# mLSTM cell and leaky-ReLU feed-forward: chunk 1 scales q on GpSimd and turns it on TensorE, k takes the gate in place of v, and chunk 0 is gated out of PSUM

## The chip, the core and the metric

One core of one Trainium2 chip runs the kernel. The metric is the device time of a run in microseconds, lower is better; the median of three runs of the kernel before is 541.46 us (541.23 to 542.38). A core has five engines that run their own instruction streams in order: TensorE (PE, with its weight loads shown apart as PEld), VectorE (DVE), ScalarE (ACT), GpSimd (POOL) and SyncE (SP), which here issues nearly all transfers. They wait for each other by semaphores. On-chip data lie in SBUF, and TensorE's results in PSUM.

## The reference

Two blocks, one after the other. The first is an mLSTM cell, batch 4, 8 heads, 768 time steps, head size 40, in f32:

```python
m_new = max(f[t] + m, i[t])                       # running maximum, per batch and head
C = exp(f[t] + m - m_new) * C + exp(i[t] - m_new) * outer(v[t], k[t])
n = exp(f[t] + m - m_new) * n + exp(i[t] - m_new) * k[t]
y[t] = sigmoid(o[t]) * (C @ q[t]) / max(|n . q[t]|, 1)
```

The second takes y as 3072 tokens of 320: `h = x @ w_in` (320 x 2048), `g = max(0.01 * h, h)`, `out = g @ w_out` (2048 x 320). The two weights come in as 64-bit floats and are turned into 32-bit ones on the chip.

## The kernel before, in words

**Chunks and steps.** The 768 time steps are cut into 6 chunks c of 128 tokens. A step s = 4 c + b is chunk c of batch b, all 8 heads; so steps 0 to 3 are chunk 0, and 4 to 7 are chunk 1. From chunk 1 on, a step's 128 tokens are two halves u of 64. A step's work on TensorE has two parts. `u_parts` makes the scores k^T q of each half (L576) and the half's contribution to the state, k^T (v times a gate) (L581); VectorE multiplies the scores by the decay matrix w (L586) and adds the contribution to the state (`state_add`, L560). Then `u_plain` (chunk 1) or `u_mix` (chunks 2 to 5) multiplies queries and weighted scores with state and values (hN, L629, or pT, L659), divides by the normaliser (L595 to L597) and applies the output gate (L640, L645). The tile `mixed(s)` holds, for each half, the weighted scores in 64 partitions and the scaled, turned q in 40 of the others, so that one matmul multiplies both with `S_v`, which holds v of the half and the state in the same way, 21 values per row of 32.

**q and k in chunk 1.** `u_split` turns k and q on TensorE by 32 small matmuls with the identity (L498), and ScalarE copies them out of PSUM (L504, four copies) to `kqT`. `prep_kq` (L484, VectorE, two instructions) multiplies the turned q by `ea`, the exponential gate per token, which must lie along the free axis in all partitions: it is written to DRAM by L298 and read back broadcast, two transfers of 128 KB a step (`spread_q`, L403). In later chunks `prep_kq` also turns k and q by VectorE transposes (L478).

**The gate of the state.** `prep_vu` (L458, GpSimd, two instructions of 64 x 336) multiplies v by exp(...) per token; the gate comes from `gT`, where `gates_T` has the gates turned to one column per batch and head (L310). GpSimd also scales the old state (`state_next`, L556) and adds the mask to w (`prep_mask`, L429).

**Chunk 0.** `u_values` multiplies values by weights into PSUM (pa, L604), VectorE copies this to `hn` (L605) and takes the denominators; `gate` (L614) reads `hn`.

**Weights.** `load_weights(n)` loads n = 0 to 3 (quarters of w_in) and n = 4 to 11 (eighths of w_out, 640 KB each), `narrow_weights` turns each to f32 by one ScalarE instruction (L231) and six on VectorE (L233, L237, L241, L243, L245, L247). They are issued in slices between the other work of chunk 0 and chunk 1, two to four per unit.

**The order.** On the four compute engines the program's order is the order written out by hand. While the feed-forward of chunk c - 1 runs as `ff_units` (for chunk 1's loop: 14 halves of L723, then 16 parts of four L758, i = 0 to 29), the cell work of chunk c is put between its units: in the loop of c = 1, `place` puts u_parts of steps 4, 5, 6, 7 behind units 2, 7, 12, 18, u_plain behind 5, 10, 15, 21, the gates of chunk 2 (`u_gates`, tg) behind 16, and the four `u_x` (which turn the result to be the next input, xt) behind 22 to 28. Narrowing comes before a unit, `ahead(s + 1)` after a step's u_plain: u_split, the exponentials of w (`prep_exp`, L437, three before each unit and the rest at u_parts), prep_kq, the loads of step s + 3, state_next, prep_vu, and the mask of the next step. L731 is the leaky ReLU on ScalarE; it frees the two PSUM banks of a unit. SP's queue is ordered by the scheduler, and at most eight transfers are under way: each waits for the one eight before it.

**PSUM.** The pool `psc` (tag c) has four banks for all cell work; a new tile takes the bank that was given up first, and TensorE waits for its last reader.

Of the kernel before, what the change touches and what calls it, by code (L numbers as in the profile page):

```python
# [18 lines left out]
def kernel(  # L19
# [26 lines left out]
    nc = tc.nc  # L46
# [239 lines left out]
    def gates_exp(c):  # L286
        bu, a, na = bus[c]
        if c == 0:
            nc.scalar.activation(bu[:, 1, :], bu[:, 0, :], AF.Exp, bias=a[:BH, P - 1 :], scale=1.0)
            return  # L290
        for u in range(2):
            at = ts(u, SL)
            last = SL * (u + 1) - 1
            nc.scalar.activation(bu[:, 2, at], a[:, at], AF.Exp, bias=na[:] if u else 0.0, scale=1.0)
            nc.scalar.activation(bu[:, 1, at], bu[:, 0, at], AF.Exp, bias=a[:, last : last + 1], scale=1.0)
        if c > 0:
            nc.sync.dma_start(a_dr[c, 0].rearrange("u n t -> n u t"), a[:].rearrange("n (u t) -> n u t", u=2))
# [9 lines left out]
    def gates_T(c, bu):  # L307
        tg = psc.tile([P, 4, BH], F32, name="tg", tag="c")
        for n in range(2):
            nc.tensor.transpose(tg[:, n, :], bu[:, n, :], ident[:BH, :BH])  # L310
        gT[c] = wk.tile([P, 2, BH], F32, name="gT")
        if c > 0:
            for u in range(2):
                last = SL * (u + 1) - 1
                nc.tensor.matmul(
                    tg[:, 2 + u, :], lhsT=bu[:, 2, last : last + 1].to_broadcast([BH, P]), rhs=ident[:BH, :BH],
                    start=True, stop=True,
                )
            gL[c] = f0[:, ts(c % 2, 2 * BH)].rearrange("p (u n) -> p u n", u=2)
        nc.vector.tensor_copy(gT[c][:], tg[:, :2, :])  # L320
        if c > 0:
            nc.vector.tensor_copy(gL[c], tg[:, 2:, :])
# [116 lines left out]
    def prep_vu(s):  # L439
# [3 lines left out]
        if s < NS:  # L443
# [11 lines left out]
            else:  # L455
                for u in range(2 if c + 1 < NB else 1):
                    rows = ts(u, SL)
                    nc.gpsimd.tensor_tensor(  # L458
                        d["vu"][rows], S_v[s % NL][rows, u, :, :, :V1], g[rows].to_broadcast([SL, H, 2, V1]), op=ALU.mult,
                    )  # L460
# [10 lines left out]
    def prep_kq(s):  # L471

        d = st[s]
        n_r = D if s < 2 * B else SL
        if s >= 2 * B:
            d["kqT"] = wk.tile([P, 2, PR * P], F32, name="kqT")
        for i in range(2 if s >= 2 * B else 0):
# [4 lines left out]
        for r in range(2):  # L482
            rows = slice(SL * r, SL * r + n_r)
            nc.vector.tensor_tensor(  # L484
                mixed(s)[rows, 1 - r], d["kqT"][rows, 1].rearrange("p (h t) -> p h t", t=SL), d["ea"][rows], op=ALU.mult,
            )

# [74 lines left out]
    def u_parts(s):  # L562
        c, b = divmod(s, B)
        d = st[s]
        kqT, w = d["kqT"], d["w"]
        run(lazy.pop(s))
# [7 lines left out]
        for h in range(H):  # L574
# [24 lines left out]
    def u_values(s):  # L599
        d = st[s]  # L600
        hn = d["hn"] = wk.tile([P, H, D1], F32, name="hn")
        pa = psc.tile([P, H, D1], F32, name="pa", tag="c")
        for h in range(H):
            nc.tensor.matmul(pa[:, h, :], lhsT=d["w"][:, h, :], rhs=d["va"][:, h, :D1], start=True, stop=True)  # L604
        nc.vector.tensor_copy(hn[:], pa[:])  # L605
        d["den"] = wk.tile([P, H], F32, name="den")
        denominators(d["den"][:], hn[:, :, D])

    def gate(s):
# [5 lines left out]
            x3, in0=d["o"].rearrange("p (h d) -> p h d", d=D), scalar=1.0, in1=d["hn"][:, :, :D],  # L615
# [181 lines left out]
    def ahead(s):  # L797

        if s < NS:
# [188 lines left out]
```

## Time and profile before

| what | value |
|---|---|
| median of three runs | 541.46 us (541.23 to 542.38) |
| profiled execution | 542.91 us, of which the span of the page is 541.1 us |
| chunk 0 on TensorE (first matmul to the start of unit 0) | 1.5 to 52.8 us |
| loop of chunk 1 | 52.8 to 149.0 us |
| loops of chunks 2 to 5 and the last feed-forward | 149.0 to 541.1 us |
| mean granted TensorE clock | 0.962 |

The profile is of one execution. The page gives busy time per engine, and the span in 40 equal slices (13.5 us each) with the busy share in tenths, TensorE's granted clock and the share of the transfer engines. Views of the trace add the instructions in order of time, busy time by stretches, the waits and who ended them, and the chain of work that ended last. L numbers are lines of the kernel before; a shape 128x320 is partitions by elements. Each f32 matmul instruction stands as two records. A busy engine need not be the bound, and an idle one matters only if the end waits for it.

### The profile page before, as it was taken

Reading aid. Unit: us, or ns where it says so; the run is one execution under the profiler, and the core shown is the slowest. Engines: PE = TensorE matmul, PEld = TensorE weight load, DVE = VectorE, ACT = ScalarE, POOL = GpSimd, SP = SyncE. Lnnn points to the kernel's source line nnn. Section 1 sums busy time; section 2 is a strip of 40 time slices with the busy share of each in tenths; the row PEclk is TensorE's granted clock in tenths of the full one; section 3 lists DMA queues with packets and bytes.
Section 4 is the critical chain, followed back from the end, with each engine's and each line's share of the span. In section 5 each row is a group of like instructions: output and inputs, shape, how many; then the busy total and the mean of one; then the engine's idle time right before and its main releaser. Section 6 shows DMA issues by size and latency. Waiting matters only on the chain.

```text
span 541.1 us, 11162 instructions
## 1 busy us (share of the span) xinstructions
PE 523.1 (97%) x4372; PEld 339.3 (63%) x4372; DVE 249.8 (46%) x443; ACT 163.3 (30%) x450; POOL 120.4 (22%) x157
## 2 busy tenths in 40 slices
PE   7989969979999999999999999999999999999997
PEld 7877858756745477645577645567654577644675
DVE  4688896999635536135527135625034532000000
ACT  4566653533433320034220043310043400022100
POOL 4134352252303332103333003423002100000000
PEclk9658988979999999999999999999999999999999
DMA  9976687977525555564655554556531121100000
GB/s 116 165 202 150 158 202 196 185 169 145 129 68 105 124 139 128 135 130 92 128 144 129 143 121 98 129 142 141 123 100 51 50 84 34 42 1 0 13 12 24
DMA packets 166003, 60.18 MB, mean 111 GB/s; under 512 B 129024, under 2 KB 156224, under 8 KB 165952
## 3 DMA queue, kind: packets, MB, share of 16 engines
q1 hardware_dynamic: 165568, 59.35, 49.6%
q8 instruction: 34, 0.56, 0.4%
q10 hardware_dynamic: 384, 0.13, 0.1%
q14 instruction: 17, 0.14, 0.1%
HBM read 52.72 MB, written 6.72 MB: 110 GB/s over the span
## 4 chain that ended last, share of the span: by engine, by line
PE 86%; DVE 6%; DMA 3%; SPq 2%; ACT 1%; issue 1%; POOL 1%; DVEq 0%; POOLq 0%; ACTq 0%
PE ph L723 37%; PE po L758 36%; PE pT L659 3%; PE sd L576 3%; DMA S<-in_v_dram 1%; PE warm L305 1%; PE sd L581 1%; PE pa L604 1%; DMA raw<-in_moe_w_out_dram 1%; PE sc L524 1%; ACT w L437 1%; PE ab L416 1%; POOL vu L458 1%; PE tkq L512 1%; DVE qn L586 1%
## 5 line engine op out<-in xcount | busy, mean ns | idle before, releaser
L723 PE MATMUL ph<-xT,w_in 64*128 64x512 f32 (+1 forms) x1120 | 218.9, 542 | 0.1
L758 PE MATMUL po<-w_out,acts 128*128 128x320 f32 x768 | 216.2, 440 | 0.0
L758 PEld LDWEIGHTS po<-w_out,acts 128*128 128x128 f32 x768 | 145.8, 193 | 60.7 <-issue 4.0
L723 PEld LDWEIGHTS ph<-xT,w_in 64*128 64x128 f32 x1120 | 108.4, 191 | 91.0 <-issue 84.2
L731 ACT ACTIVATE acts<-ph 128x512 f32<-128x512 f32 (+1 forms) x112 | 54.0, 534 | 153.6 <-PE ph L723 153.5
L586 DVE TENSOR_TENSOR qn<-w,sd 64x512 f32<-64x512 f32 x40 | 27.4, 685 | 122.7 <-PE sd L581 87.8
L556 POOL TENSOR_TENSOR S<-S,f 40x336 f32<-40x336 f32 x36 | 28.8, 800 | 181.3 <-PE pT L659 135.9
L437 ACT ACTIVATE w<-w,gT 128x64 f32<-128x64 f32 (+1 forms) x192 | 52.4, 350 | 1.0 <-DVE w L423 1.0
L484 DVE TENSOR_TENSOR qn<-kqT,ea 64x512 f32<-64x512 f32 (+1 forms) x40 | 30.2, 755 | 4.7 <-ACT kqT L504 3.4
L458 POOL TENSOR_TENSOR vu<-S,gT 64x336 f32<-64x336 f32 x36 | 31.4, 871 | 2.7
L673 POOL TENSOR_TENSOR xb<-xb,den 128x320 f32<-128x320 f32 x16 | 11.6, 727 | 88.5 <-DVE xb L670 88.5
L766 ACT COPY y<-po 128x320 f32<-128x320 f32 x12 | 5.1, 425 | 86.7 <-PE po L758 86.7
L766 ACT COPY hn<-po 128x320 f32<-128x320 f32 x12 | 5.1, 425 | 86.3 <-PE po L758 86.3
L576 PEld LDWEIGHTS sd<-kqT 40*64 40x64 f32 x640 | 21.1, 138 | 12.8 <-issue 10.5
L666 DVE STREAM_TRANSPOSE hb<-pT 128x512 f32<-128x512 f32 x16 | 11.5, 717 | 38.1 <-PE pT L659 38.1
L429 POOL TENSOR_TENSOR w<-w,i 128x512 f32<-128x512 f32 x20 | 27.3, 1365 | 7.9 <-ACT acts L731 6.5
L581 PE MATMUL sd<-vu,kn 64*40 64x42 f32 x576 | 21.2, 218 | 4.0 <-POOL vu L458 4.0
L576 PE MATMUL sd<-kqT 40*64 40x64 f32 x640 | 24.2, 225 | 0.4 <-DVE S L560 0.2
L659 PEld LDWEIGHTS pT<-qn,S 128*64 128x64 f32 x512 | 16.2, 138 | 10.5 <-issue 6.9
L581 PEld LDWEIGHTS sd<-vu,kn 64*40 64x40 f32 x576 | 18.6, 114 | 4.2 <-POOL vu L458 4.2
L677 DVE STREAM_TRANSPOSE x<-xb 128x512 f32<-128x512 f32 x16 | 17.7, 1104 | 7.8 <-POOL xb L673 7.8
L478 DVE STREAM_TRANSPOSE kqT<-rb 128x512 f32<-128x512 f32 x32 | 20.6, 680 | 0.0
(123 smaller groups left out, 362.4 us busy)
## 6 DMA issues: line engine op xcount, KB each, us to landing
w<-a_dr SPq DMA_DIRECT2D x40, 128.0 KB
ea<-a_dr SPq DMA_DIRECT2D x40, 128.0 KB
rb<-in_k_dram SPq DMA_DIRECT2D x64, 80.0 KB
rb<-in_q_dram SPq DMA_DIRECT2D x64, 80.0 KB
rb<-in_o_gate_dram SPq DMA_DIRECT2D x64, 80.0 KB
kn<-in_k_dram SPq DMA_DIRECT2D x24, 160.0 KB
raw<-in_moe_w_out_dram SPq DMA_DIRECT2D x6, 640.0 KB
S<-in_v_dram SPq DMA_DIRECT2D x80, 40.0 KB
```

Source lines behind the costliest of these rows:

```text
L429: nc.gpsimd.tensor_tensor(w, w, cm2.unsqueeze(1).to_broadcast([P, H, SL]), op=ALU.add)
L437: yield nc.scalar.activation(w[:, h, :], w[:, h, :], AF.Exp, bias=gT[c][:, 0, bh : bh + 1], scale=1.0)
L458: nc.gpsimd.tensor_tensor(d["vu"][rows], S_v[s % NL][rows, u, :, :, :V1], g[rows].to_broadcast([SL, H, 2, V1]), op=ALU.mult,)
L484: nc.vector.tensor_tensor(mixed(s)[rows, 1 - r], d["kqT"][rows, 1].rearrange("p (h t) -> p h t", t=SL), d["ea"][rows], op=ALU.mult,)
L556: nc.gpsimd.tensor_tensor(new, old, g, op=ALU.mult)
L576: nc.tensor.matmul(bank[1 - u][toks, h, :], lhsT=kqT[rows, 0, ts(h, SL)], rhs=kqT[rows, 1, ts(h, SL)], start=True, stop=True,)
L581: nc.tensor.matmul(dC[u][:, h].rearrange("p k d -> p (k d)"), lhsT=d["k"][toks, h, :D], rhs=d["vu"][toks, h].rearrange("p k d -> p (k d)") ...
L586: nc.vector.tensor_tensor(mixed(s)[toks, u], w[toks], bank[1 - u][toks], op=ALU.mult)
L659: nc.tensor.matmul(pT[DP * r : DP * (r + 1), j * P + u * SL : j * P + (u + 1) * SL], lhsT=S[:, u, h, :], rhs=m[:, u, h, :], start=True, st ...
L723: nc.tensor.matmul(ph[r][:, cols], lhsT=w_row(r, slot, j), rhs=xT[DP * r : DP * (r + 1), slot, cols], start=(slot == 0), stop=(slot == KC ...
L731: nc.scalar.activation(acts[:, f, cols], ph[r][:, cols], AF.Prelu, alpha=0.01)
L758: nc.tensor.matmul(po[n][:], lhsT=acts[:, f, ts(n, P)], rhs=w_out[:, f, :], start=(f == 0), stop=(f == NF - 1),)
```

## The change

- In chunk 1 the gate that was `ea` is turned by `gates_T` as a third kind into `gT`. `prep_qs` (GpSimd) multiplies the rows of q, as loaded, by it, into a tile of the ring `y`; `split_qs` (TensorE, 16 matmuls with the identity, into two more tiles of the pool) turns them at the start of u_parts, and ScalarE copies both halves into `mixed(s)`. VectorE's product, the transfers of `ea` for steps 4 to 7 and the write of that gate to DRAM go.
- From chunk 1 on, k and not v takes the gate of the state: one GpSimd product 128 x 320 in place of two of 64 x 336; the matmul takes v in place from `S_v`.
- In chunk 0, denominators and gate read pa in PSUM; the copy to `hn` goes.

```diff
@@ gates_exp
-            nc.sync.dma_start(a_dr[c, 1].rearrange("u n t -> n u t"), bu[:, 2, :].rearrange("n (u t) -> n u t", u=2))
+            if c > 1:
+                nc.sync.dma_start(a_dr[c, 1].rearrange("u n t -> n u t"), bu[:, 2, :].rearrange("n (u t) -> n u t", u=2))
@@ gates_T
-        tg = psc.tile([P, 4, BH], F32, name="tg", tag="c")
-        for n in range(2):
+        tg = psc.tile([P, 5, BH], F32, name="tg", tag="c")
+        kinds = 3 if c == 1 else 2
+        for n in range(kinds):
             nc.tensor.transpose(tg[:, n, :], bu[:, n, :], ident[:BH, :BH])
...
-        nc.vector.tensor_copy(gT[c][:], tg[:, :2, :])
+        nc.vector.tensor_copy(gT[c][:, :kinds], tg[:, :kinds, :])
@@ prep_vu
-                for u in range(2 if c + 1 < NB else 1):
-                    rows = ts(u, SL)
-                    nc.gpsimd.tensor_tensor(
-                        d["vu"][rows], S_v[s % NL][rows, u, :, :, :V1], g[rows].to_broadcast([SL, H, 2, V1]), op=ALU.mult,
-                    )
+                d["ku"] = d["vu"][:].rearrange("p h k d -> p (h k d)")[:, : H * D].rearrange("p (h d) -> p h d", d=D)
+                nc.gpsimd.tensor_tensor(
+                    d["ku"], d["k"][:, :, :D], gT[c][:, 1, ts(b, H)].unsqueeze(2).to_broadcast([P, H, D]), op=ALU.mult,
+                )
+
+    def prep_qs(s):
+        c, b = divmod(s, B)
+        d = st[s]
+        d["qs"] = wk.tile([P, Dm], F32, name="y")[:].rearrange("p (h d) -> p h d", d=D)
+        nc.gpsimd.tensor_tensor(
+            d["qs"], natural(s, 1), gT[c][:, 2, ts(b, H)].unsqueeze(2).to_broadcast([P, H, D]), op=ALU.mult,
+        )
@@ after prep_kq (which now serves chunks 2 to 5 alone)
+    def split_qs(s):
+        tq = [psc.tile([P, H, SL], F32, name=f"tq{u}", tag="c") for u in range(2)]
+        for h in range(H):
+            for u, toks, rows in subs(s):
+                nc.tensor.matmul(tq[u][rows, h, :], lhsT=st[s]["qs"][toks, h], rhs=ident[toks, toks], start=True, stop=True)
+        for u, toks, rows in subs(s):
+            nc.scalar.copy(mixed(s)[rows, u], tq[u][rows])
@@ u_parts
+        if c == 1:
+            split_qs(s)
         run(lazy.pop(s))
...
-                        dC[u][:, h].rearrange("p k d -> p (k d)"), lhsT=d["k"][toks, h, :D],
-                        rhs=d["vu"][toks, h].rearrange("p k d -> p (k d)"), start=True, stop=True,
+                        dC[u][:, h].rearrange("p k d -> p (k d)"), lhsT=d["ku"][toks, h],
+                        rhs=S_v[s % NL][toks, u, h, :, :V1], start=True, stop=True,
@@ u_values, gate
-        hn = d["hn"] = wk.tile([P, H, D1], F32, name="hn")
-        pa = psc.tile([P, H, D1], F32, name="pa", tag="c")
+        pa = d["pa"] = psc.tile([P, H, D1], F32, name="pa", tag="c")
...
-        nc.vector.tensor_copy(hn[:], pa[:])
-        denominators(d["den"][:], hn[:, :, D])
+        denominators(d["den"][:], pa[:, :, D])
...
-            x3, in0=d["o"].rearrange("p (h d) -> p h d", d=D), scalar=1.0, in1=d["hn"][:, :, :D],
+            x3, in0=d["o"].rearrange("p (h d) -> p h d", d=D), scalar=1.0, in1=d["pa"][:, :, :D],
@@ ahead
-            prep_kq(s)
+            if s < 2 * B:
+                prep_qs(s)
+            else:
+                prep_kq(s)
...
-                spread_q(s + NR)
+                if s + NR >= 2 * B:
+                    spread_q(s + NR)
@@ before the loop
         for s in (B, B + 1):
             feed(s)
-            spread_q(s)
```

More of the change, by code (lines that the diff above doesn't have):

```diff
@@ L307, in gates_T @@
     def gates_T(c, bu):
-        tg = psc.tile([P, 4, BH], F32, name="tg", tag="c")
-        for n in range(2):
+        tg = psc.tile([P, 5, BH], F32, name="tg", tag="c")
+        kinds = 3 if c == 1 else 2
+        for n in range(kinds):
             nc.tensor.transpose(tg[:, n, :], bu[:, n, :], ident[:BH, :BH])
-        gT[c] = wk.tile([P, 2, BH], F32, name="gT")
+        gT[c] = wk.tile([P, 3, BH], F32, name="gT")
         if c > 0:
@@ L315, in gates_T @@
                 nc.tensor.matmul(
-                    tg[:, 2 + u, :], lhsT=bu[:, 2, last : last + 1].to_broadcast([BH, P]), rhs=ident[:BH, :BH],
+                    tg[:, 3 + u, :], lhsT=bu[:, 2, last : last + 1].to_broadcast([BH, P]), rhs=ident[:BH, :BH],
                     start=True, stop=True,
@@ L319, in gates_T @@
             gL[c] = f0[:, ts(c % 2, 2 * BH)].rearrange("p (u n) -> p u n", u=2)
-        nc.vector.tensor_copy(gT[c][:], tg[:, :2, :])
+        nc.vector.tensor_copy(gT[c][:, :kinds], tg[:, :kinds, :])
         if c > 0:
-            nc.vector.tensor_copy(gL[c], tg[:, 2:, :])
+            nc.vector.tensor_copy(gL[c], tg[:, 3:, :])
     st = {}
@@ L473, in prep_kq @@
         d = st[s]
[L474 to L477, printed above, removed]
+        d["kqT"] = wk.tile([P, 2, PR * P], F32, name="kqT")
+        for i in range(2):
             nc.vector.transpose(
@@ L482, in prep_kq @@
         for r in range(2):
-            rows = slice(SL * r, SL * r + n_r)
+            rows = ts(r, SL)
             nc.vector.tensor_tensor(
```

## The prediction

> **What bounds the kernel now.** I read the page's busy rows and its forty slices first:
>
> ```profile
> PE 523.1 (97%) x4372; PEld 339.3 (63%) x4372; DVE 249.8 (46%) x443; ACT 163.3 (30%) x450; POOL 120.4 (22%) x157
> PE   7989969979999999999999999999999999999997
> DVE  4688896999635536135527135625034532000000
> PEclk9658988979999999999999999999999999999999
> DMA  9976687977525555564655554556531121100000
> ```
>
> TensorE is busy to the end, but "busy" counts matmuls at half clock. From slice 11 (149 us) on, TensorE is full at full clock, and the edit adds nothing there. So the question is when chunk 1 ends. Its slices (4 to 10) are those in which VectorE is at eight or nine tenths. The stretches are cut finer next; columns are busy time (with counts) of TensorE, its weight loads, VectorE, ScalarE, GpSimd, then clock, DMA share, GB/s:
>
> ```profile
> 60.00:70.00 10.00, 10.00 (x223) 8.77 (x222) 9.77 (x17) 5.08 (x14) 2.23 (x2) 1.00 0.74 186
> 70.00:80.00 10.00, 5.66 (x61) 4.53 (x61) 9.73 (x12) 6.14 (x17) 4.84 (x5) 0.92 0.90 191
> 80.00:90.00 10.00, 10.00 (x120) 8.36 (x114) 8.61 (x13) 1.98 (x5) 1.24 (x1) 0.74 0.61 126
> 110.00:120.00 10.00, 7.65 (x20) 5.30 (x21) 9.67 (x16) 2.44 (x9) 5.72 (x6) 0.66 0.74 164
> 150.00:470.00 320.00, 320.00 (x2646) 190.61 (x2644) 128.62 (x235) 78.20 (x228) 66.54 (x79) 1.00 0.47 108
> ```
>
> TensorE stands idle at 70 to 80 and at 110 to 120, and after each gap its clock is low. VectorE is full in both. The timelines of TensorE, VectorE and GpSimd say why (start, length, line; bracket: idle before and releaser):
>
> ```profile
> 73.55 0.16 DVE L595 TENSOR_SCALAR den<-hN 128x8 f32<-128x8 f32 x1
> 74.06 0.43 DVE L640 SCALAR_TENSOR_TENSOR x<-rb,hN 128x320 f32<-128x320 f32 x1
> 75.07 2.01 DVE L484 TENSOR_TENSOR qn<-kqT,ea 40x512 f32<-40x512 f32 x2
> ...
> 112.24 0.51 DVE L560 TENSOR_TENSOR S<-S,sd 40x336 f32<-40x336 f32 x1
> 112.78 2.02 DVE L484 TENSOR_TENSOR qn<-kqT,ea 40x512 f32<-40x512 f32 x2
> ```
> ```profile
> 74.64 0.72 POOL L645 TENSOR_TENSOR x<-x,den 128x320 f32<-128x320 f32 x1 [4.75 <-DVE x L640]
> 76.61 3.07 POOL L458 TENSOR_TENSOR vu<-S,gT 64x336 f32<-64x336 f32 x2
> ```
> ```profile
> 112.35 0.28 PE L310 MATMUL tg<-ident,bu 32*128 32x32 f32 x2 [3.30 <-DVE hn L640]
> 113.36 7.55 PE L758 MATMUL po<-w_out,acts 128*128 128x320 f32 x16
> ```
>
> hN of step 4 was done on TensorE at 69.0, but VectorE, in order behind weight narrowing, read it only at 73.55. So GpSimd's L645 and everything behind it (state, vu) came late, and TensorE's sd waited for vu until 79.74: 5.1 us. The second gap has the same cause: tg takes hN's bank and waits for L640.
>
> **What the Trainium skill says.** "TensorE: Matmul & The Clock Gate", Part 1: about 3.4 us of idling put the array at half clock, as long sustained work takes it back. The trace agrees: after 3.30 us idle, 16 L758 matmuls took 7.55 us, against 4.57 at 100 us. The same page, Part 3 (row/col tiling): small matmuls in different strips of the array run side by side; here 64 L498 transposes pass in 1.03 us. "GPSIMD Engine Reference", 1. Specifications: GpSimd shares its SBUF interfaces with VectorE and contends with instructions of two SBUF inputs. Agrees: L458 takes 0.80 alone at its shortest, 1.10 and 1.91 at 76.6.
>
> **Part by part.**
> - *VectorE's product, chunk 1.* L484 goes for steps 4 to 7: 1.87 + 2.01 + 1.86 + 2.02 = 7.8 us of VectorE, all in its full stretch, and the waits in front of two of them (1.46 and 1.97 us, for ScalarE's L504).
> - *Query by TensorE.* Per step 16 matmuls of L498's form (32 records): 1.03 / 2 = 0.52 us of TensorE, 2.1 in all, straight on its path. Two ScalarE copies, L504's form: 1.17 us a step. ScalarE is 46 of 97 us busy here; but they stand ahead of the last two exponentials of the step, which VectorE's L586 awaits: 1.2 us there, which is why I put L586 of steps 5 to 7 late by that. GpSimd: one 128x320 product, L645's form, 0.72 alone, up to 1.17 (L618 beside VectorE).
> - *k instead of v.* Two 64x336 L458 (2.05 to 3.07 us a step) become one 128x320 product, 0.72 to 1.17. With the query's product GpSimd stays at about its former length. TensorE's rhs is now v in place, rows of 21 at stride 32 instead of dense. hN reads exactly that already (128x42, 233 ns mean against 218). I take no extra cost. Bounds: 0, and hN's own rate, 1.06/32 = 33 ns per record against 1.07/64 = 17.
> - *Chunk 0.* Four L605 copies (0.50 us) go; the two readers take PSUM, and L640 shows that price (0.44 against 0.48). The bank is held until the gate. The order of waits gives dC(2) and tkq(3) other banks: tkq(3) waits for L528 at 30.4, +0.15 us. VectorE's stretch then runs into a wait for ScalarE's L231 (0.91 at 53.93), so only the last gate counts: the first chunk-1 matmul comes 0.4 us earlier. The third transpose of the gates is 0.12 us.
> - *Transfers.* Eight ea loads of 128 KB and one a_dr write leave SP's queue before the slices at 200 GB/s are over. A pair takes 1.23 us of queue: by step 6's q SP is 3.0 us ahead (two pairs and 0.5). But the queue's order changes too: the last w_out load (n=11, 116.91) now has ea(9), k(10), w(10) and three k blocks ahead of it.
>
> **The walk.** TensorE's L723 start at 52.4. VectorE no longer waits for L504: L237 begins at 54.4 instead of 58.21, it is full until L586 of step 4 (sd ends 61.0, 0.35 idle), L247 ends 64.5, narrowing until 70.4, L640 of step 4 ends 71.4 instead of 74.5. GpSimd: L645 0.7, q 1.0, state 1.1, k 1.1: k ready at 75.4. TensorE reaches split and sd of step 5 at 74.5, and ends them at 76.3, before: 81.50. No idle window, so the next 60 matmuls take 6.73 and not 8.54: hN(5) starts at 83.05, before: 90.05, 7.0 earlier. VectorE is there (L640 of step 5 at 84.8). TensorE: tk, two halves, split and sd of step 6 end at 91.3. L586 of step 6 waits for the exponentials behind the copies: 93.0, before: 101.55. VectorE then needs the same 10.66 us to the end of L640: 103.7, before 112.21, 8.5 earlier. TensorE had come to tg at 102.1: a gap of 1.6 us instead of 3.3, at full clock. VectorE's next stretch (112.21 to L586 of step 7 at 127.18) lacks L484: 14.97 - 2.05 = 12.9, so L586 starts at 116.6 and L560 ends 1.93 later, 118.5. TensorE would be at hN(7) at 117.2, so 1.4 us idle, and hN(7) starts at 118.6 against 129.16: **10.6 us earlier**. From there on, TensorE's work is the same: 8 output parts and 4 xt, 18.7 us. The last narrowing must end before the parts that read it, at 128.9: VectorE gets there at 127.8, with the raw load landed by about 121 (3.9 MB between n=9 and it at the 172 GB/s of before). Then 541.1 - 10.6 = 530.5 of span. The profiled execution took 542.91, 1.8 over its span and 1.45 over the median; taken off the median, 541.46 - 10.6 = **530.9**.
>
> **Rivals.**
> 1. *The weights' transfers become the bound.* DMA moves 214 GB/s at 91 to 106. If n=9 and n=10 land where they did (108), L247 of step n=9 can't end before about 113, and only the first gap's 7 us and little else is kept: 534 to 537. Against it: queue 3 to 5 us ahead. 0.16.
> 2. *All gaps close.* Idle and slow clock of 52 to 149 are 0.5 + 5.1 + 2.5 + 3.3 + 3.6 + 0.5 = 15.5; less 2.1 of splits, plus 0.4: 13.8 off, 527.7. It needs VectorE to be no longer last at hN(7). 0.08.
> 3. *The chain on GpSimd stays last.* If q, state and k take 1.9 each beside VectorE (L458's worst), k of step 5 is at 77.8 (72.1 + 5.7), and TensorE idles at its gap again: 3 to 5 off, 537. For: three in a row; against: L484, itself two SBUF inputs, no longer contends. 0.06.
> 4. *The stall moves, nothing is won* (each gap is taken over by ScalarE's added copies): within 0.2%. Against: ScalarE idle for half the stretch. 0.04.
> 5. *Slower: the strided v.* 448 L581 records lie in chunks 2 to 5, where TensorE is full. At hN's rate they would cost 7.7 us more, still faster: 538. From 25 ns more per record the kernel is slower; if the two token halves also stopped running side by side (17 to 67 ns), 448 x 0.05 = 22 us: 553. For: no row shows this form with 64 rows. Against: hN's reads. 0.08.
>
> That the change does not do what it says is no rival: the built program's order of instructions shows every removal and addition.
>
> **How the numbers follow.** The forecast, 528.5 to 533 by itself, has 0.58. What a measurement can tell from no change is 0.2%, 1.1 us. Faster: 0.58 + 0.16 + 0.08 + 0.06 = 0.88; same 0.04; slower 0.08. The range takes in rivals 1 and 2 with the forecast, 0.82: 527 to 537. It covers a half-clock window after one of the short gaps, +2.5 us.
>
> **What would show it.** hN of step 5 at 83 and of step 7 at 118 to 119; no low clock at 76 to 90; 16 L758 after tg in under 5 us; no L484 before 110; sd of chunks 2 to 5 still 1.07 us. Wrong if sd lengthens there, or if ScalarE's L231 waits for raw in 95 to 110.

## The result, and the profile after

| | before | changed |
|---|---|---|
| median | 541.42 us (541.23 to 542.38) | 533.59 us (533.21 to 534.19) |
| profiled execution | 542.91 us, span 541.1 us | 533.48 us, span 531.7 us |
| mean granted TensorE clock | 0.962 | 0.98 |

The ratio of the times is 0.9853, with a 95% interval of 0.9836 to 0.987: 7.8 us faster, where 10.6 were forecast. The time is inside the range of 527 to 537, 2.7 us above the forecast of 530.9 and just outside the likeliest case's own range of 528.5 to 533. Line numbers are now those of the changed kernel: hN is L646, the gate L657 and L662, the weighted scores L605, the sum of the state L577, sd L595 and L600, the two feed-forward matmuls L740 and L775, the scaled query L468 (GpSimd), its split L501 (TensorE) and L503 (ScalarE), and the scaled k L459.

The page of the changed kernel, busy rows and slices:

```profile
PE 517.3 (97%) x4501; PEld 334.5 (63%) x4501; DVE 241.1 (45%) x431; ACT 168.0 (32%) x458; POOL 111.1 (21%) x145
...
PE   7879989999999999999999999999999999999997
...
DVE  4788998999055526055616055614054432000000
...
PEclk9768999999999999999999999999999999999999
```

Slices are counted from 0. The clock is full from slice 4 on, so both low-clock places of chunk 1 (slices 5, 6 and 8 before) are gone, and in chunk 1 TensorE is short of nine tenths only in slice 5. VectorE is still at eight or nine tenths in slices 2 to 9: chunk 1 has the same bound, with less to do. The stretches, in the columns of the prediction:

```profile
60.00:70.00 10.00, 10.00 (x191) 8.78 (x184) 9.73 (x10) 5.90 (x16) 2.60 (x2) 1.00 0.86 252
70.00:80.00 10.00, 8.35 (x154) 7.19 (x152) 9.06 (x14) 6.56 (x18) 5.67 (x5) 1.00 0.68 106
80.00:90.00 10.00, 10.00 (x172) 8.78 (x170) 7.97 (x15) 6.39 (x15) 3.99 (x5) 1.00 0.83 212
110.00:120.00 10.00, 9.35 (x133) 6.86 (x133) 9.73 (x12) 1.16 (x2) 4.24 (x4) 1.00 0.79 134
...
139.56:531.70 392.14, 388.94 (x2931) 229.77 (x2930) 127.55 (x235) 89.16 (x249) 58.07 (x69) 1.00 0.40 92
```

TensorE's idle time at 70 to 80 fell from 4.3 to 1.65 us, and the clock stayed at 1.00. The last line begins where chunk 1's last output part ends; the same stretch of the kernel before begins at 149.0:

```profile
149.00:541.10 392.10, 388.95 (x2931) 230.18 (x2930) 128.62 (x235) 89.01 (x249) 66.54 (x79) 1.00 0.39 91
```

392.10 against 392.14 us, with 388.95 and 388.94 us of TensorE: chunks 2 to 5 are untouched to a twentieth of a microsecond, so all 9.4 us of span were won before the end of chunk 1. That also settles rival 5: v read in place costs TensorE nothing.

The 9.4 us fall into two parts. Below, "the loop" is the time from VectorE's first L233 of chunk 1's loop to hN of step 7, once its wait is over. First before, then changed:

```profile
53.93 0.92 DVE L233 TENSOR_SCALAR w_in<-w_in 128x1280 f32<-128x1280 f32 x1 [0.91 <-ACT w_in L231]
129.16 1.13 PE L629 MATMUL hN<-S,qn 128*64 128x42 f32 x30 [0.28 <-DVE S L560]
```
```profile
52.22 1.30 DVE L233 TENSOR_SCALAR w_in<-w_in 128x1280 f32<-128x1280 f32 x1 [1.20 <-ACT w_in L231]
119.72 1.10 PE L646 MATMUL hN<-S,qn 128*64 128x42 f32 x30 [0.65 <-DVE S L577]
```

The loop took 129.16 - 53.93 = 75.2 us before and 119.72 - 52.22 = 67.5 us changed, 7.7 us less. The other 1.7 us is its earlier start.

The timelines of the changed kernel at the two places of the gaps (start, length; bracket: idle before and releaser):

```profile
71.36 0.44 DVE L657 SCALAR_TENSOR_TENSOR x<-rb,hN 128x320 f32<-128x320 f32 x1
71.83 0.51 DVE L577 TENSOR_TENSOR S<-S,sd 40x336 f32<-40x336 f32 x1
72.37 1.64 DVE L247 TENSOR_TENSOR w_in<-w_in,raw 128x1280 f32<-128x1280 f32 x1
...
71.95 0.72 POOL L662 TENSOR_TENSOR x<-x,den 128x320 f32<-128x320 f32 x1 [2.35 <-DVE x L657]
72.63 1.97 POOL L468 TENSOR_TENSOR y<-rb,gT 128x320 f32<-128x320 f32 x1
74.68 0.90 POOL L573 TENSOR_TENSOR S<-S,f 40x336 f32<-40x336 f32 x1
75.65 0.85 POOL L459 TENSOR_TENSOR vu<-kn,gT 128x320 f32<-128x320 f32 x1
...
74.65 1.09 PE L501 MATMUL tq<-ident,y 64*40 64x64 f32 x32 [0.95 <-POOL y L468]
...
76.56 0.30 PE L600 MATMUL sd<-S,vu 64*40 64x42 f32 x3 [0.70 <-POOL vu L459]
...
104.99 0.28 PE L312 MATMUL tg<-ident,bu 32*128 32x32 f32 x2 [0.73 <-DVE hn L657]
...
105.64 4.57 PE L775 MATMUL po<-w_out,acts 128*128 128x320 f32 x16
```

At step 5 the gate is read at 71.36 instead of 74.06, and k is scaled by 75.65 + 0.85 = 76.50 (v was by 79.7). TensorE waits 0.95 and 0.70 us. Before, its waits there were 0.24, 2.28 and 1.71 us, 4.2 in all; the gap of 5.1 us in the prediction counts the few small matmuls between them as well. The two long ones:

```profile
77.76 0.27 PE L581 MATMUL sd<-vu,kn 64*40 64x42 f32 x2 [2.28 <-POOL vu L458]
79.74 0.29 PE L581 MATMUL sd<-vu,kn 64*40 64x42 f32 x1 [1.71 <-POOL vu L458]
```

At tg the wait is 0.73 instead of 3.30 us, and the 16 matmuls behind it take 4.57 us instead of 7.55.

### The profile page after: what moved, and what is told of

Its sections match the earlier page's. It is cut to its first block, busy times and chain, and to the rows that moved or that the text cites. A ratio compares the mean times of both kernels' runs of the same rounds, so it can differ in the third digit from the quotient of the medians.

```text
span 531.7 us, 11350 instructions
## 1 busy us (share of the span) xinstructions
PE 517.3 (97%) x4501; PEld 334.5 (63%) x4501; DVE 241.1 (45%) x431; ACT 168.0 (32%) x458; POOL 111.1 (21%) x145
## 4 chain that ended last, share of the span: by engine, by line
PE 81%; DVE 7%; SPq 6%; DMA 2%; ACT 2%; issue 1%; POOL 1%; ACTq 0%; DVEq 0%; POOLq 0%
PE po L775 36%; PE ph L740 36%; PE pT L676 3%; SPq L213 3%; PE sd L595 3%; SPq L338 2%; DVE raw L245 1%; SPq L352 1%; PE sd L600 1%; DVE qn L605 1%; DVE w_out L247 1%; DMA rb<-in_q_dram 1%; DVE w_out L241 1%; DVE raw L243 1%; DMA raw<-in_moe_w_in_dram 1%
## 5 line engine op out<-in xcount | busy, mean ns | idle before, releaser
L740 PE MATMUL ph<-xT,w_in 64*128 64x512 f32 (+1 forms) x1120 | 217.3, 538 | 0.6 <-ACT acts L748 0.6
L775 PE MATMUL po<-w_out,acts 128*128 128x320 f32 x768 | 213.3, 435 | 0.0
L775 PEld LDWEIGHTS po<-w_out,acts 128*128 128x128 f32 x768 | 143.8, 190 | 59.7 <-issue 1.8
L740 PEld LDWEIGHTS ph<-xT,w_in 64*128 64x128 f32 x1120 | 107.1, 189 | 91.1 <-issue 84.4
L605 DVE TENSOR_TENSOR qn<-w,sd 64x512 f32<-64x512 f32 x40 | 27.4, 686 | 125.6 <-PE sd L600 90.1
L573 POOL TENSOR_TENSOR S<-S,f 40x336 f32<-40x336 f32 x36 | 30.7, 854 | 187.8 <-PE pT L676 146.8
L431 POOL TENSOR_TENSOR w<-w,i 128x512 f32<-128x512 f32 x20 | 26.7, 1333 | 10.2 <-DMA w<-a_dr 10.1
L595 PEld LDWEIGHTS sd<-kqT 40*64 40x64 f32 x640 | 20.3, 135 | 10.8 <-issue 9.3
L595 PE MATMUL sd<-kqT 40*64 40x64 f32 x640 | 23.0, 221 | 0.0
L492 DVE TENSOR_TENSOR qn<-kqT,ea 64x512 f32<-64x512 f32 x32 | 22.4, 701 | 1.1
L600 PE MATMUL sd<-S,vu 64*40 64x42 f32 x576 | 20.6, 215 | 0.7 <-POOL vu L459 0.7
L600 PEld LDWEIGHTS sd<-S,vu 64*40 64x40 f32 x576 | 18.2, 111 | 0.8 <-POOL vu L459 0.8
L577 DVE TENSOR_TENSOR S<-S,sd 40x336 f32<-40x336 f32 x36 | 18.1, 503 | 0.9
```

The source lines that it names most:

```text
L431: nc.gpsimd.tensor_tensor(w, w, cm2.unsqueeze(1).to_broadcast([P, H, SL]), op=ALU.add)
L492: nc.vector.tensor_tensor(mixed(s)[rows, 1 - r], d["kqT"][rows, 1].rearrange("p (h t) -> p h t", t=SL), d["ea"][rows], op=ALU.mult,)
L573: nc.gpsimd.tensor_tensor(new, old, g, op=ALU.mult)
L595: nc.tensor.matmul(bank[1 - u][toks, h, :], lhsT=kqT[rows, 0, ts(h, SL)], rhs=kqT[rows, 1, ts(h, SL)], start=True, stop=True,)
L600: nc.tensor.matmul(dC[u][:, h].rearrange("p k d -> p (k d)"), lhsT=d["ku"][toks, h], rhs=S_v[s % NL][toks, u, h, :, :V1], start=True, stop ...
L605: nc.vector.tensor_tensor(mixed(s)[toks, u], w[toks], bank[1 - u][toks], op=ALU.mult)
```

## The experiments

Each kernel was timed beside the kernel before, in three sets: 542.57 us (query alone to product left out), 544.61 us (chunk 0 put back to early query product; single executions from 541.9 to 546.22) and 542.14 us (the rest). Differences within a set are what counts. The changed kernel itself stands only in the third set, so a comparison of the second set with it crosses sets; there the four kernels are compared with each other too. Line numbers in the views are each kernel's own. The first set takes the change apart.

**The query alone.** The changed kernel, with the k product and chunk 0 put back:

```diff
-                d["ku"] = ...; nc.gpsimd.tensor_tensor(d["ku"], d["k"][:, :, :D], gT..., op=ALU.mult)
+                for u in range(2 if c + 1 < NB else 1): ... nc.gpsimd.tensor_tensor(d["vu"][rows], S_v..., g..., op=ALU.mult)
-        denominators(d["den"][:], pa[:, :, D])
+        nc.vector.tensor_copy(hn[:], pa[:]); denominators(d["den"][:], hn[:, :, D])
```

> The changed kernel with the k product and the chunk-0 gating put back as they were: only the query's path is changed. Theory (the gain is VectorE's freed 7.8 us in chunk 1, at the price of 1.04 us of TensorE a step): 534.5 to 537, that is 4.5 to 7 us under the kernel before, L484 gone before 110 us and the low-clock stretch after step 5 shorter or gone. Rival 'GpSimd': with the query's product (0.7 to 2.0 us) added to the old vu products (2.1 to 3.1 us) GpSimd's chain decides at step 5, sd(5) starts no earlier than before (79.7) and the whole is 539 to 541. Rival 'chunk 0': under 2 us of gain here, since the gain is the earlier start of chunk 1.

Measured: 539.02 us, ratio 0.9925 (0.99 to 0.9951), 3.6 us faster. The time is above the 534.5 to 537 of the theory and on the edge of the rival's 539 to 541, so GpSimd carries more of the gap than I had given it. Its stretches at step 5:

```profile
70.00:80.00 10.00, 7.74 (x174) 6.60 (x166) 8.06 (x11) 7.29 (x19) 7.34 (x7) 0.92 0.55 82
80.00:90.00 10.00, 10.00 (x101) 8.23 (x96) 6.23 (x10) 2.33 (x7) 0.28 (x1) 0.74 0.77 202
```

VectorE is down to 8.06 and 6.23 us busy; the cover has gone to GpSimd, with 7.34. TensorE still idles 2.3 us at step 5 and then runs at 0.74 of its clock. This kernel also drops the ea transfers, which cost the changed kernel 1.2 to 1.9 us when they are put back (below), so part of the 3.6 us may be theirs.

**k alone.** The kernel before, with k scaled in place of v:

```diff
-                        dC..., lhsT=d["k"][toks, h, :D], rhs=d["vu"][toks, h]...
+                        dC..., lhsT=d["ku"][toks, h],    rhs=S_v[s % NL][toks, u, h, :, :V1]
```

> The kernel before with k scaled in place of v, nothing else. Theory: VectorE's order is unchanged, so the two gaps stay; GpSimd's product behind step 4's gate falls from 3.1 us to about 1, so TensorE's wait for it at 77 to 80 us shortens by about 2 us, and of that 1 to 2 us reach the end: 539.5 to 540.5. Rival 'GpSimd relief is the gain': 536 or less. Rival of the prediction, strided v costs TensorE: sd of chunks 2 to 5 longer than 1.07 us a step, above 541.5.

Measured: 538.60 us, ratio 0.9921 (0.9889 to 0.9953), 4.0 us faster: more than the 1 to 2 us of the theory, and as much as the query alone. (In its trace the loop is 126.27 - 53.56 = 72.7 us, 2.5 less than before.) GpSimd's last product at step 5 took 1.05 us, in place of 3.07; but VectorE's product still stands in the chain, and sd still waits. The wait at tg stays as well, at 2.97 us.

```profile
77.83 0.36 PE L580 MATMUL sd<-S,vu 64*40 64x42 f32 x3 [2.24 <-POOL vu L457]
...
75.18 2.01 DVE L483 TENSOR_TENSOR qn<-kqT,ea 40x512 f32<-40x512 f32 x2
```

**Chunk 0 alone.** The kernel before, with pa read in PSUM:

```diff
-        nc.vector.tensor_copy(hn[:], pa[:])
-        denominators(d["den"][:], hn[:, :, D])
+        denominators(d["den"][:], pa[:, :, D])
```

> The kernel before with chunk 0 gated out of PSUM, nothing else. The changed kernel's first chunk-1 matmul on TensorE came 2.2 us earlier than before where 0.4 was forecast. If the gating makes that, the first chunk-1 matmul comes at 50.5 to 51 here; but VectorE is the last at both gaps, and its L484 of step 4 waits for ScalarE: 0.5 to 1.5 us gained at the end, 540 to 541. If the early start has another cause (the start of the run, the later chunk-1 order), it stays at 52.4 or later and the time within 0.5 us of before. Rival 'chunk 0 is the gain': 537 or less.

Measured: 542.39 us, ratio 0.9999 (0.9979 to 1.0019): nothing, where 0.5 to 1.5 us were expected. In the trace TensorE reached the xt transpose ahead of chunk 1 at 48.11 instead of 50.21, and then met the first query's transfer:

```profile
52.54 0.33 PE L498 MATMUL tk<-ident,rb 64*40 64x64 f32 x2 [3.65 <-DMA rb<-in_q_dram]
...
52.50:60.00 7.50, 7.46 (x106) 6.60 (x108) 3.21 (x5) 4.74 (x14) 2.39 (x3) 0.78 0.63 182
```

2.1 us earlier became a wait of 3.65 us, and the clock fell to 0.78 behind it. But this is the slowest of twelve executions, 545.42 us, 3 us over the median, so how long the wait is in an ordinary one is not shown. The three parts alone sum to 3.6 + 4.0 + 0.2 = 7.8 us, as much as the whole change gained. With intervals of 2.7 to 5.4, 2.5 to 6.0 and -1.0 to 1.1 us, and with two parts that shorten the same wait, this does not show that they add.

**The product left out.** The kernel before without VectorE's L484 in chunk 1:

```diff
-        for r in range(2):
+        for r in range(2 if s >= 2 * B else 0):
             nc.vector.tensor_tensor(mixed(s)[rows, 1 - r], d["kqT"]..., d["ea"][rows], op=ALU.mult)
```

> The kernel before with VectorE's product L484 left out in chunk 1 and nothing in its place: the queries of chunk 1 are not scaled, that part of the computation is left out; ea is still loaded, v still scaled. Theory: this has VectorE's relief without the split's TensorE and ScalarE time, but keeps the 3.1 us of vu on GpSimd: 530 to 534. If it comes no lower than 538, VectorE's product was not what held chunk 1. If it comes below 529, the TensorE split costs more on the path than its 4.1 us of busy time.

Measured: 537.11 us, ratio 0.9897 (0.9857 to 0.9937), 5.5 us faster and short of the theory's 530 to 534. With all 7.8 us of VectorE's work gone and nothing in its place, step 5 looks like this:

```profile
76.08 0.36 PE L581 MATMUL sd<-vu,kn 64*40 64x42 f32 x2 [2.64 <-POOL vu L458]
...
73.16 1.90 POOL L556 TENSOR_TENSOR S<-S,f 40x336 f32<-40x336 f32 x1
75.13 1.87 POOL L458 TENSOR_TENSOR vu<-S,gT 64x336 f32<-64x336 f32 x2
...
70.00:80.00 10.00, 6.74 (x100) 5.57 (x98) 8.47 (x12) 4.87 (x15) 5.33 (x5) 0.79 0.89 154
...
107.50 0.28 PE L310 MATMUL tg<-ident,bu 32*128 32x32 f32 x2 [1.10 <-DVE hn L640]
...
108.15 4.57 PE L758 MATMUL po<-w_out,acts 128*128 128x320 f32 x16
```

The gate's product begins on GpSimd at 72.36, but state and vu behind it take until 77, TensorE idles 3.26 us, and the next 60 feed-forward matmuls take 8.63 us, as before. So relief of VectorE alone does not close this gap: behind VectorE stands GpSimd's chain, and each part of the change shortens another piece of the same wait. The second gap, at tg, does close with it: the wait is 1.10 instead of 3.30 us, and the 16 matmuls behind it run at full clock.

**Chunk 0 put back into the changed kernel.** The four copies return, q and k stay changed (diff: that of chunk 0 alone, reversed).

> The changed kernel with chunk 0's copies out of PSUM put back (q and k changed, chunk 0 as before). Theory from the sums: q alone gained 3.6 us and k alone 4.0, chunk 0 alone nothing, because TensorE, 2.1 us earlier, waited 3.65 us for the first query transfer. If that holds in the changed kernel too, this is 533 to 534.3. Rival: without the ea transfers in the queue the first query is early enough, so the earlier start of chunk 1 is kept there, and putting the copies back costs 1 to 2.2 us: 534.6 to 536.

Measured: 534.23 us (533.27 to 534.85), against 533.59 and, in a later set, 534.14 of the changed kernel. The profiled span was 532.9 us, 1.2 more than the changed kernel's, and VectorE's first L233 of the chunk-1 loop began at 53.37 instead of 52.22. The medians are too close to call it: chunk 0 is worth 0 to 1 us. The loop took 120.88 - 53.37 = 67.5 us, as in the changed kernel, so the 1.2 us lie ahead of it. That start also moves by itself. Over all traces here this first L233 begins at 52.58 to 53.93 us in the five kernels with the copies (mean 53.4) and at 51.80 to 54.54 in the nine without (mean 53.0): 0.5 us between the means, and 2.7 between kernels whose chunk 0 is the same.

**The transfers kept.** The changed kernel with the ea loads and the write of that gate issued as before, and read by nothing:

```diff
-            if c > 1:
+            if c > 0:
                 nc.sync.dma_start(a_dr[c, 1]...)
-                if s + NR >= 2 * B:
-                    spread_q(s + NR)
+                spread_q(s + NR)
             feed(s)
+            spread_q(s)
```

> The changed kernel with the ea transfers of chunk 1 (eight loads of 128 KB, one write) issued as before and read by nothing. Theory: the first query of chunk 1 lands about 2 us later and TensorE's first tk waits for it, 1 to 2 us of that reach VectorE's stretch; the later queue is not the bound: 534 to 536, with ScalarE's waits for weights (L231) under 1 us before 110. Rival 1 of the prediction (the transfers become the bound): the gain rests on the dropped loads, 537 to 541 here, with TensorE or VectorE waiting for raw between 95 and 115 us. No role for transfers at all: 533.2 to 534.

Measured: 535.45 us (534.18 to 537.38), 1.3 to 1.9 us above the two medians of the changed kernel, as the theory said, and 1.2 and 1.9 above chunk 0 put back and the early query product in its own set. Where it goes, in timelines and one stretch of its slowest execution:

```profile
52.76 0.25 PE L515 MATMUL tk<-ident,rb 64*40 64x64 f32 x2 [1.96 <-DMA rb<-in_q_dram]
...
64.45 1.40 DVE L605 TENSOR_TENSOR qn<-w,sd 64x512 f32<-64x512 f32 x2 [2.15 <-ACT qn L503]
...
52.50:60.00 7.50, 7.24 (x102) 6.25 (x104) 6.44 (x12) 5.64 (x13) 5.82 (x4) 0.77 0.60 179
```

The first query lands late again, the clock falls to 0.77, and VectorE, which ran through here in the changed kernel, waits 2.15 us for step 4's split. The loop, 123.48 - 53.76 = 69.7 us, is longer by 2.2. The late query is no chance: in all five traces with ea loads TensorE waited for it 0.77 to 3.65 us, until 50.70 to 52.76; in the nine without, at most 0.79 us, and where it waited at all, until 49.59 to 50.46. The weights have no part in it: VectorE's longest wait for narrowing's first step (L231) between 60 and 110 us is 0.41 us, so rival 1 finds no support even with these loads in the queue.

**The split issued twice.**

```diff
-        for h in range(H):
+        for h in [*range(H), *range(H)]:
             ... nc.tensor.matmul(tq[u][rows, h, :], lhsT=st[s]["qs"][toks, h], rhs=ident[toks, toks], ...)
```

> The changed kernel with every split matmul (tq) issued twice, same result. A split takes 1.03 to 1.09 us for 32 records. Theory: it is on the path at steps 4 to 6 through the exponentials behind its copies, hidden in part at step 5 (TensorE waits 0.70 us for ku after it) and wholly at step 7 (TensorE waits for VectorE there): 1.5 to 3 us slower than the changed kernel, 535 to 536.6. If the whole split stands on the path as the prediction put it: 4.1 us, 537.7. If it is hidden: within 0.7 us, 533 to 534.3.

Measured: 535.18 us (535.05 to 537.45), 1.0 to 1.6 us slower than the changed kernel, and than chunk 0 put back and the early query product in its own set, for 0.9 us more of TensorE in each of four steps (62 records in 1.93 us). VectorE's waits show how much came through:

```profile
62.60 1.40 DVE L605 TENSOR_TENSOR qn<-w,sd 64x512 f32<-64x512 f32 x2 [0.93 <-ACT qn L503]
...
95.49 1.40 DVE L605 TENSOR_TENSOR qn<-w,sd 64x512 f32<-64x512 f32 x2 [1.17 <-ACT w L439]
```

At step 4 the wait is new, at step 5 it is 1.44 instead of 0.68 us, and at step 6 1.17 instead of 0.52. On TensorE the second split of step 5 lies in time that was idle, and at step 7 nobody waits for it. The wait of step 4 does not reach the next gate: L657 comes 72.00 - 53.24 = 18.8 us after the loop's start, 19.1 in the changed kernel, because narrowing met less of GpSimd in between. The loop took 121.10 - 53.24 = 67.9 us, and 67.5 in the changed kernel. So of the 3.7 us added, 0.4 (by the traces) to 1.6 us (by the medians) reach the end, less than half.

**GpSimd's query product earlier.** In the changed kernel, steps 5 to 7:

```diff
-            if s < 2 * B:
+            if s == B:
                 prep_qs(s)
...
+                    if fn is u_parts and s + 1 < 2 * B:
+                        prep_qs(s + 1)
```

> The changed kernel with GpSimd's query product of steps 5 to 7 issued one stage earlier, ahead of the gate of the step before, so that it is not in GpSimd's chain behind that gate. In the changed kernel's step 5 TensorE waited 0.95 us for the query's product (1.97 us long) and 0.70 us for ku. Theory: both waits go and sd(5) ends 1.2 to 1.6 us earlier; VectorE, which waited 0.68 us there, then decides, so 0.5 to 1.3 us are gained: 532.3 to 533.1. Rival: VectorE and ScalarE are the only path and nothing changes, 533.4 to 534. Slower if GpSimd waits for the query's transfer at step 6 or 7 with the gate's product queued behind it: 534.5 or more.

Measured: 533.55 us (532.98 to 534.12): across sets no difference to the changed kernel, as the rival had it. GpSimd's timeline:

```profile
66.61 1.30 POOL L468 TENSOR_TENSOR y<-rb,gT 128x320 f32<-128x320 f32 x1
...
73.90 1.89 POOL L573 TENSOR_TENSOR S<-S,f 40x336 f32<-40x336 f32 x1
75.87 0.85 POOL L459 TENSOR_TENSOR vu<-kn,gT 128x320 f32<-128x320 f32 x1
```

The query's product is out of the chain, but now the state's takes 1.89 us instead of 0.90. Whichever instruction follows the gate's product on GpSimd starts beside VectorE's L247 and takes 1.9 us; so TensorE's two waits became one of 1.18 us. VectorE did run through at step 5, and at step 6 it then waited 0.92 us for an exponential.

**The changed kernel again, and its copies behind the exponentials.** The second:

```diff
-            split_qs(s)
+            tq = split_qs(s)
         run(lazy.pop(s))
+        if c == 1:
+            for u, toks, rows in subs(s):
+                nc.scalar.copy(mixed(s)[rows, u], tq[u][rows])
```

> The changed kernel itself, beside the three others of this set, so that they can be compared with it under the same conditions: 533.2 to 534.3.

> The changed kernel with ScalarE's two copies of the split put behind the last exponentials of the step instead of ahead of them. In the changed kernel VectorE's L605 of step 6 waited 0.52 us for an exponential that stood behind the 1.19 us of copies. Theory: the exponentials come 1.2 us earlier, VectorE runs through, and 0.3 to 0.6 us are gained: 533.0 to 533.3. Rival: the next wait (L605 for sd on TensorE) stands right behind it and nothing is gained: 533.5 to 534.

Measured: 534.14 (533.31 to 535.38) and 534.02 us (532.49 to 534.64). L605 of step 6 no longer waits in the second one, and its loop took 119.99 - 53.12 = 66.9 us against 67.5; but the times do not separate the two, and the 0.3 to 0.6 us of the theory are not shown. The repeated trace is of more use. Its waits at step 5 are those of the first (0.99 and 0.69 against 0.95 and 0.70 us); the same stretch of both, the changed kernel first:

```profile
76.00:80.00 4.00, 3.44 (x82) 3.16 (x84) 3.26 (x5) 1.43 (x4) 1.77 (x2) 1.00 0.68 90
```
```profile
76.00:80.00 4.00, 3.59 (x68) 3.21 (x70) 2.53 (x4) 1.28 (x4) 1.62 (x2) 0.57 0.79 123
```

The same idle time was followed by full clock once and by 0.57 the other time, and the execution took 535.38 instead of 533.48 us.

**Three moves together.** The early query product, the late copies, and half of the split's heads turned to the other half of the columns:

```diff
+                out_rows = rows if h % 2 == 0 else slice(SL * u, SL * u + D)
-                nc.tensor.matmul(tq[u][rows, h, :], ...)
+                nc.tensor.matmul(tq[u][out_rows, h, :], ...)
...
+            for odd in range(2): nc.scalar.copy(mixed(s)[rows, u, odd::2, :], tq[u][out_rows, odd::2, :])
```

> The changed kernel with three moves together: GpSimd's query product one stage earlier, the copies behind the exponentials, and every second head of the split put to the other half of the columns, so that four 64x40 matmuls are side by side as in the tk transposes (32 records in about 0.55 us instead of 1.03). Theory: L605 of steps 5 and 6 no longer wait (0.68 and 0.52 us), TensorE's split shrinks by 0.5 us a step where it counts: 532.0 to 533.1. Rival: VectorE alone sets chunk 1 by now and the moves take time from engines that wait anyway: 533.4 to 534.

Measured: 533.32 us (533.15 to 533.55), ratio 0.9835 (0.9817 to 0.9853), the lowest of the kernels that compute everything, but its interval overlaps that of the changed kernel beside it, 0.9844 (0.9825 to 0.9864): a gain is not shown. The split does shrink:

```profile
91.34 0.66 PE L502 MATMUL tq<-ident,y 64*40 64x64 f32 x32
```

0.66 against 1.03 us, and the loop took 119.52 - 54.54 = 65.0 us, 2.5 less. But chunk 0 of this execution ended 2.3 us later, at half clock from 30 to 40 us (0.50, where the changed kernel's trace had 0.67). It is the latest start of all traces; whether that is chance or comes with the kernel stays open.

**The query's scaling left out of the changed kernel.**

```diff
-        if c == 1:
-            split_qs(s)
...
-            if s < 2 * B:
-                prep_qs(s)
-            else:
+            if s >= 2 * B:
                 prep_kq(s)
```

> The changed kernel with the scaled query of chunk 1 left out altogether (no GpSimd product, no split on TensorE, no copies; the queries that multiply the state are whatever the buffer held, so that part of the computation is left out). The difference to the changed kernel is the whole price of the replacement for VectorE's product. Theory from doubling the split (1.5 us) and the waits seen (0.52 and 0.68 us on VectorE): 1.5 to 2.5 us, 531 to 532.2. If the split's 4.1 us of TensorE all count: 529.5. If the replacement is hidden: 533 to 534.

Measured: 531.18 us (530.33 to 533.16), ratio 0.98 (0.9771 to 0.9829), 3.0 us below the changed kernel in the same set. So what took VectorE's product over gives back about 3 of 11 us; the theory said 1.5 to 2.5. The loop agrees, in the slowest execution of this kernel: 119.35 - 53.02 = 66.3 us, and 121.10 - 52.03 = 69.1 in the changed kernel's repeated trace, both with a low clock after step 5. Without the query TensorE still waits once at step 5, for 2.00 us, with GpSimd's state product at 1.89 us again.

## Why the prediction was right, and where it was not

**What bounds chunk 1: right, with one piece left out of the words.** I read both gaps as VectorE's lateness passed on. The second is that: VectorE's stretch from L657 of step 6 to L605 of step 7 took 117.65 - 104.87 = 12.8 us, forecast 12.9, and the 16 matmuls behind tg ran at full clock. With the product alone gone the wait at tg fell from 3.30 to 1.10 us; with k alone it stayed at 2.97. The first is VectorE's lateness plus GpSimd's chain: with the product alone gone, TensorE still idles 3.26 us. The walk did count that chain (0.7, 1.0, 1.1, 1.1), but in the parts I gave k in place of v no gain ("GpSimd stays at about its former length"). Alone it is worth 4.0 us. The walk had it right because it used the short k; as a statement on which edit pays, it was wrong.

**The walk, term by term.**

| event | forecast | measured |
|---|---|---|
| L237 of step 4 starts | 54.4 | 53.55 |
| L657 of step 4 ends | 71.4 | 71.80 |
| k of step 5 scaled | 75.4 | 76.50 |
| hN of step 5 starts | 83.05 | 84.31 |
| L605 of step 6 | 93.0 | 94.05 |
| L657 of step 6 ends | 103.7 | 104.85 |
| L605 of step 7 | 116.6 | 117.65 |
| hN of step 7 waits until | 118.6 | 119.72 |

The walk looks 0.4 us off ahead of step 5, and 1.1 to 1.3 from there to the end. But the trace had started 0.85 us early. From L237 of step 4 to hN of step 7 the walk has 118.6 - 54.4 = 64.2 us and the trace 119.72 - 53.55 = 66.2, so 2.0 us were lost: 1.25 ahead of the gate of step 4, and the rest between it and hN of step 5.

Ahead of the gate it was VectorE's narrowing. The walk took over its lengths from the kernel before, but it now met GpSimd at other places:

```profile
64.80 1.78 DVE L237 TENSOR_SCALAR w_in<-w_in 128x1280 uint32<-128x1280 uint32 x1
...
64.60 1.29 POOL L431 TENSOR_TENSOR w<-w,i 128x512 f32<-128x512 f32 x1 [9.20 <-DMA w<-a_dr]
```

Before, this L237 took 0.83 us; in the trace of the split issued twice, where the mask (L431) had ended 2.1 us ahead of it, it took 0.83 again. So here GpSimd slowed VectorE; below it is the other way round.

Behind the gate two terms were too small. GpSimd's query product took 1.97 us, where I put 1.0; and the split took 1.09, where I put 0.52. The groups of the changed kernel in the loop (count, busy, mean ns, idle before):

```profile
L459 POOL TENSOR_TENSOR vu<-kn,gT 128x320 f32<-128x320 f32 x6 | 6.0, 996 | 0.5
L468 POOL TENSOR_TENSOR y<-rb,gT 128x320 f32<-128x320 f32 x4 | 5.0, 1240 | 0.0
...
L503 ACT COPY qn<-tq 40x512 f32<-40x512 f32 x8 | 4.7, 581 | 5.2 <-PE tq L501 5.1
L501 PE MATMUL tq<-ident,y 64*40 64x64 f32 x128 | 4.4, 218 | 0.9 <-POOL y L468 0.9
```

*GpSimd.* My upper price of 1.17 us came from a row beside VectorE, but not beside the 128x1280 sum L247, which has two inputs in SBUF. The Trainium skill ("GPSIMD Engine Reference", 1. Specifications) says that such instructions contend with GpSimd. The trace agrees and gives the size: the same product takes 0.72 us at its shortest and 1.97 beside L247. The early product showed that it is a price of the place, not of the instruction: moved away, it hit the state's product instead (0.90 to 1.89). In eleven traces the GpSimd instruction that began beside this L247 (1.64 us) ended 0.58 to 0.63 us after it, a little less than its own shortest time in this loop (0.72 us for the query's product, 0.76 for the state's): it looks as if it waited until L247 was over. That is read from the times, not shown by an edit. (The shortest L458 before was 0.76 us, not the 0.80 of the prediction.)

*The split.* I took half of the 1.03 us in which 64 tk transposes pass. But tk uses four combinations of row half and column half, and the split's halves use two. The Trainium skill ("TensorE: Matmul & The Clock Gate", Part 3) says that small matmuls run side by side when they lie in different tiles of the array, so what counts is how many tiles are in use. The traces agree: 32 records on two of the four combinations took 1.03 us, on all four (three moves) 0.66. The price was twice my figure, 4.2 us of TensorE in sum. That doubling it cost the end less than half of what it added fits with TensorE's waits at steps 5 and 7, where it idles anyway; my "straight on its path" was too strict.

**Chunk 0 and the transfers.** I put 0.4 us for chunk 0 and nothing for the first transfers. In the changed kernel's trace the first chunk-1 feed-forward matmul came at 50.61, 1.8 us before my 52.4. The copies do not explain that. Against the trace of before, TensorE reached the last xt transpose of chunk 0 2.1 us earlier in chunk 0 alone, but only 0.2 us earlier (50.02 against 50.21) with the transfers kept, which has no copies either. Over all traces their absence brings the loop's start 0.5 us forward, near my 0.4; the rest is scatter, of unknown cause. The transfers were the term that I left out: with ea loads ahead of it in the queue the first query comes late in every trace, and keeping them costs 1.2 to 1.9 us. I had listed what SP gains by step 6 and not looked at step 4.

**From the span to the median.** The span fell by 541.1 - 531.7 = 9.4 us, the profiled executions by 9.4 and the medians by 7.8. The execution of before lay 1.5 us above its median, that of the changed kernel 0.1 below, and I took the gain of a walk through the first off the median. The gain inside the loop, 7.7 us, is as large as that of the medians. The other 1.7 us of span are the early start, of which the experiments give about 0.5 to the copies. So the miss lies in the loop: I forecast 10.6 us with 0.4 of chunk 0, that is 10.2 for the loop, and it gave 7.7. That the walk's end came within 1.2 us (10.6 against 9.4) of the trace was in part luck: the early start hid half of the error.

**The rivals.** The weights as a bound (1) did not come: ScalarE's L231 of the last load waited 11.04 us for raw, but until 123.55, outside the 95 to 110 that I had named, and the last L247 ended at 128.98, close to my 127.8. Not all gaps closed (2): 0.95, 0.70, 0.73 and 0.65 us stay. GpSimd last (3) came in part, and is one of the two places where the walk lost its time. The stall that only moves (4) fell by the 7.8 us, and the strided v (5) by the 392.1 us of chunks 2 to 5.

## What to carry to other kernels

A gap that one engine's lateness opens can be held open by a second engine standing right behind it: taking work off the first alone gained 5.5 us here, the shorter chain on the second alone 4.0, and the two with what was added 7.8. When work is moved onto TensorE as small matmuls, price it by how many tiles of the array its operands and outputs reach, and spread the outputs over both column halves (0.66 instead of 1.03 us a step here, though no gain in the time was shown). When an edit moves GpSimd's instructions in time against VectorE's, take neither's lengths from the kernel before. When the spans of two traces are compared, cut them into stretches and look at the same stretch in all traces at hand: here 1.7 of 9.4 us lay ahead of the loop, most of that scatter.

## What the hardware showed beyond the forecast

TensorE's clock went down after much shorter idling than the 3.3 us of the kernel before. Idle time of TensorE between 70 and 80 us, and the granted clock of the two stretches 70 to 80 and 80 to 90, over all traces (in chunk 0 alone and transfers kept the gap reaches to 80.3 and is counted whole):

| kernel | idle, us | clock |
|---|---|---|
| before | 4.3 | 0.92, 0.74 |
| chunk 0 alone | 3.6 | 0.98, 0.68 |
| product left out | 3.3 | 0.79, 0.87 |
| k alone | 3.1 | 0.85, 0.80 |
| query alone | 2.3 | 0.92, 0.74 |
| query's scaling left out | 2.0 | 0.83, 1.00 |
| changed, again | 1.7 | 0.83, 1.00 |
| changed; chunk 0 put back; copies late; transfers kept | 1.6 to 1.7 | 1.00, 1.00 |
| early product; three moves; split twice | 1.2; 0.7; 0 | 1.00, 1.00 |

At 2 us and more each of these traces lost the clock, at 1.6 to 1.7 one of five, at 1.2 and less none. The idle time ahead of hN of step 7 fits: after waits of 1.01 and 0.94 us (product left out) and 0.96 and 0.94 (chunk 0 alone) the next 8 matmuls took 3.93 and 3.90 us, after 0.70 and 0.97 (query alone) 2.42, which is their time at full clock. The Trainium skill ("TensorE: Matmul & The Clock Gate", Part 1) says that activity is judged in a window of about 3.4 us that runs freely and does not start with the kernel. That the same 1.7 us led to both outcomes fits this. Its table names a whole idle window as what brings the low clock; these traces show it after less. One such loss, between two executions of the changed kernel, goes with 1.9 us of time, and with a loop of 69.1 instead of 67.5 us.
